# A new schedule for the same 807 operations of a long-convolution block with its feed-forward network

## The chip, the cores and the metric

The kernel runs on one core of a Trainium2 chip. A core has four compute engines with instruction streams of their own, here called PE (TensorE, matmuls out of SBUF into PSUM), ACT (ScalarE), DVE (VectorE) and POOL (GpSimd), and SP (SyncE), which in this kernel only issues DMA transfers. The profile lists PE's weight loads apart, as PEld. The metric is device microseconds of one launch.

## The reference

One sequence of S = 2048 tokens with D = 640 channels, all in bfloat16. Part A is a convolution block in the manner of H3, part B a SwiGLU network of width F = 1728 (`B_x` isn't used).

```python
x   = A_q
lnq = layernorm(x)
k_s = sum over t < 4 of shift(k, 3 - t rows down) * shift_k[:, 3 - t]   # causal, per channel
kv  = k_s * v
y   = irfft(rfft(kv, 4096) * rfft(ssm_k.T, 4096))[:2048] + kv * ssm_D   # per channel
h   = x + lnq * y
n   = layernorm(h)
out = h + (silu(n @ w_gate) * (n @ w_up)) @ w_down
```

## The kernel before

**Tiling.** The sequence is cut into four chunks i = 0 to 3 of 512 tokens, the filter ssm_k into four blocks m likewise. Each is transformed with a DFT matrix (`tab`, 128 rows) by matmuls; the long convolution is the sum of spectral products of chunk and block. `SEQ` names the order in which the tasks are recorded: "P01 K W F0 S1 P11 I1 P02 P12 P03 P13 F1 S2 P22 I2 P23 F2 S3 P33 I3 F3" (P products of chunk and block, I inverse transform, F the feed-forward network (FFN), S the forward side of a chunk, K the fourth filter block, W the FFN's weights).

**Tasks.** The Python code records 807 operations ("tasks") with their reads and writes in a graph `g`; a task's number is the order in which it was recorded. The code gives each a name. Those that matter here:

- k0t / k0e: PE transposes of the first chunk of k and their PSUM evacuations (L528; `evac`, L455 on ACT, L457 or L458 on DVE); tload kT (L450): DMA transposes of the later chunks of k.
- tp, ke, kv: the shift taps as matmuls with diagonals (L732), their evacuation (L455), the product with v (L748, L755). v0 to v3 are the loads of v, x0 to x3 those of q.
- kt / kte, kf / kfe: transposes of the filter to KT and their evacuation; forward transform of the filter (L581) and its evacuation. kb and kc: butterflies and combinations on DVE (L561).
- xf / xfe: forward transform of kv (L581, L619) and its evacuation; p: spectral products (L783); yb: butterflies before the inverse transform (L561, L651).
- iv i.p with a letter: inverse transform of chunk i, position p: the matmuls (L939, L944), e evacuation (L954), g the multiply and add (L961), m and s mean and squares on ACT (L860, L862), v and r the reciprocal deviation (L855 on DVE, L857 on POOL), n the normalised tile (L1001 on DVE).
- ht: the DMA transpose of a normalised tile into hnT, the FFN's input (L450).
- fu and fg i.hg: up and gate matmuls of half h (256 tokens), group g (L1049); sg, su, sv their evacuations (L1057, L1062); mu the product (L1070); dn the down projection (L1135, the last ones split, L1012); gd a copy of its input.
- rs: evacuation of dn (L1151 on ACT, L1152 on DVE), ra: the accumulating DMA that adds it to h, issued by POOL (L568); out: the store, issued by SP (L1164).
- la, lp: small steps of the first layer norm's statistics. UA, GA, UB, GB, PKg, PKu, WdA to WdD: weight loads; itab: the table of the inverse transform.

**Order.** Nothing about order is decided by the graph: `PLAN` holds, for each engine, the list of task numbers that it executes in turn. Each engine runs its list in order, and waits at the head of a task until everything that it depends on is done; whatever stands behind it in the list waits too. SP's list orders the issue of DMAs, so a store whose data isn't ready holds up the transfers behind it.

**PSUM.** There are four PSUM tiles of two banks each. The string `units` in the plan says which of the four each of the successive uses takes. `arrange` then adds, for every use, a wait on the readers of the one that had the tile before:

```python
        for t in self.order["pe"]:
            for pt in t.opens:
                prev = last.get(pt.unit)
                if prev is not None:
                    t.pre |= {x for x in prev.users if x.eng != "pe"}
                last[pt.unit] = pt
```

So a matmul group waits for its data and for the evacuation of the former content of its tile, which ACT or DVE does. `emit` turns dependencies between engines into semaphore waits. A task may run on any engine in its list `engs`; most evacuations may go to ACT or DVE.

Of the kernel before, what the change touches and what calls it, by code (L numbers as in the profile page):

```python
# [50 lines left out]
class _Graph:  # L51
# [131 lines left out]
    def emit(self, block):  # L183
# [74 lines left out]

PLAN = {
# [8 lines left out]
    "act":  # L268
# [9 lines left out]
    "dve":  # L278
# [9 lines left out]
    "pool":  # L288
        "18 16 14 15 128 177 168 161 201 195 186 200 227 229 228 340 285 360 361 398 370 371 289 380 390 293 403 391 381 297 "
        "408 417 419 466 420 525 470 559 474 550 568 478 577 680 584 589 701 706 694 695 635 728 719 639 737 746 643 647 ",  # L290
    "sp":
        "0 2 3 8 4 6 9 7 234 10 12 13 239 300 238 11 230 235 301 233 232 231 299 237 481 179 170 197 188 236 286 482 373 363 "
        "290 294 298 383 650 393 480 467 651 561 552 570 475 471 479 579 649 730 721 640 739 748 644 648 794 800 636 797 803 "
        "806 ",
    "units":
        "0113201022031012033321231021332312133313321010001232312221313201230311022320230103301222001112012120120312322323013103"
        "23101021312302023330210213103130021301200122003201320321302",
    "fills": {
        "wb0": ["zmem", 3],
        "k0t4.0": ["zmem", 1],  # L300
# [945 lines left out]
```

## Time and profile before

| | us |
|---|---|
| three runs | 254.22, 254.73, 254.75 (median 254.73) |
| the profiled execution, whole | 254.13 |
| its span in the profile | 252.2 |

The page of the profile gives the engines' busy time; TensorE's granted clock was full all along. Most of the bytes go out through two kinds of queues: q1, issued by SP, 23.56 MB, and q0, issued by POOL, 13.11 MB. A group in the list of costliest groups has one line of the code, one engine and one operation, with the busy time, the mean of one, and the idle time of the engine just ahead. The largest:

| group | count | busy us | mean ns |
|---|---|---|---|
| L1135 PE matmul (down projection) | 420 | 58.4 | 300 |
| L783 DVE (spectral products) | 29 | 45.1 | 1576 |
| L1049 PE matmul, hnT with GB | 280 | 34.2 | 273 |
| L1057 ACT (activation of the gate) | 32 | 29.0 | 913 |
| L581 PE matmul (forward transforms) | 128 | 19.4 | 300 |

Times of a timeline's row are the start in the span, then the duration; a row with "x4" puts four neighbours of one kind together. A landing time counts from the issue of a DMA to the arrival of its last packet.

### The profile page before, as it was taken

What the parts mean: (1) busy time and instruction counts of PE and PEld (TensorE: products, weight loads), DVE (VectorE), ACT (ScalarE), POOL (GpSimd) and SP (SyncE); (2) the same over time, 40 slices, a digit from 0 to 9 for tenths busy, and PEclk for the clock granted to TensorE, in tenths of its full rate; (3) what the DMA queues carried; (4) which work ended last, traced back from release to release, by engine and by line L of the source; (5) the groups of instructions that cost most, each with busy time, mean ns of one, the idle gap of its engine ahead of it and who ended that gap; (6) DMA issues with size and microseconds to landing.
All of it is one profiled execution on the core that took longest, in us unless ns stands there. A gap on an engine that the chain in (4) does not pass through costs nothing.

```text
span 252.2 us, 5601 instructions
## 1 busy us (share of the span) xinstructions
PE 243.4 (96%) x2405; PEld 190.7 (76%) x2405; DVE 195.5 (78%) x249; ACT 184.7 (73%) x303; POOL 58.7 (23%) x62
## 2 busy tenths in 40 slices
PE   7998997999999999999999999999999999999995
PEld 3776574688887867888888765888886678888763
DVE  2899999999989999999999896989959321312322
ACT  2499999999897994678999699478982856543500
POOL 1000033443113457602103333211141122100000
PEclk9999999999999999999999999999999999999999
DMA  6999999989994465999914718795871144300003
GB/s 212 338 316 222 389 381 292 142 154 169 274 176 78 141 104 109 174 169 216 208 19 76 189 26 82 169 232 99 146 140 26 23 85 79 81 0 3 0 29 104
DMA packets 39063, 37.04 MB, mean 147 GB/s; under 512 B 21235, under 2 KB 34046, under 8 KB 39038
## 3 DMA queue, kind: packets, MB, share of 16 engines
q1 hardware_dynamic: 31648, 23.56, 35.0%
q0 software_dynamic: 7376, 13.11, 30.7%
q8 instruction: 19, 0.31, 0.5%
q14 instruction: 6, 0.05, 0.0%
q10 hardware_dynamic: 14, 0.01, 0.0%
HBM read 16.29 MB, written 2.62 MB: 75 GB/s over the span
## 4 chain that ended last, share of the span: by engine, by line
PE 73%; DVE 11%; DMA 8%; ACT 5%; issue 1%; SPq 0%; DVEq 0%
PE ps L1049 45%; PE ps L1135 18%; PE ps L581 4%; DMA kvo<-in_A_v_dram 3%; DVE C L561 2%; PE ps L944 2%; DVE tt L783 2%; DMA hnT<-qo 2%; PE ps L1012 2%; DMA k0n<-in_A_k_dram 2%; PE ps L732 1%; DVE kvo L755 1%; DVE Y L783 1%; DMA xh<-RB 1%; DVE kvo L748 1%
## 5 line engine op out<-in xcount | busy, mean ns | idle before, releaser
L1135 PE MATMUL ps<-Wd,gu 128*128 128x320 bf16 (+1 forms) x420 | 58.4, 300 | 0.3 <-ACT qo L954 0.3
L1135 PEld LDWEIGHTS ps<-Wd,gu 128*128 128x128 bf16 (+1 forms) x420 | 38.9, 97 | 18.7 <-issue 2.8
L783 DVE TENSOR_TENSOR tt<-XH,C 128x2560 bf16<-128x2560 bf16 (+1 forms) x29 | 45.1, 1576 | 0.2
L1070 DVE TENSOR_TENSOR gu<-gu,ub 128x1024 bf16<-128x1024 bf16 (+1 forms) x32 | 19.9, 621 | 20.9 <-ACT gu L1057 12.9
L1057 ACT ACTIVATE gu<-ps 128x1024 bf16<-128x1024 f32 (+1 forms) x32 | 29.0, 913 | 8.7 <-PE ps L1049 8.5
L1049 PE MATMUL ps<-hnT,GB 128*128 128x256 bf16 x280 | 34.2, 273 | 0.0
L1049 PE MATMUL ps<-hnT,UB 128*128 128x256 bf16 x280 | 33.7, 273 | 0.0
L1062 ACT ACTIVATE ub<-ps 128x1024 bf16<-128x1024 f32 x24 | 24.5, 1020 | 12.4 <-PE ps L1049 9.7
L1049 PEld LDWEIGHTS ps<-hnT,UB 128*128 128x128 bf16 x280 | 27.4, 98 | 3.3
L1049 PEld LDWEIGHTS ps<-hnT,GB 128*128 128x128 bf16 x280 | 27.2, 98 | 3.3
L1049 PE MATMUL ps<-hnT,UA 128*128 128x256 bf16 x240 | 28.8, 273 | 0.0
L1049 PE MATMUL ps<-hnT,GA 128*128 128x256 bf16 x240 | 28.2, 273 | 0.4 <-DMA hnT<-qo 0.4
L1049 PEld LDWEIGHTS ps<-hnT,GA 128*128 128x128 bf16 x240 | 23.4, 98 | 3.5 <-DVE OS L458 0.8
L1049 PEld LDWEIGHTS ps<-hnT,UA 128*128 128x128 bf16 x240 | 23.3, 98 | 3.1 <-ACT XH L455 0.2
L857 POOL TENSOR_TENSOR mv<-mv,half 128x1 f32<-128x1 f32 x16 | 15.7, 982 | 32.9 <-DVE mv L855 28.5
L581 PE MATMUL ps<-KT,tab 128*128 128x320 bf16 x128 | 19.4, 300 | 2.3 <-DVE KT L457 1.1
L860 ACT ACTIVATE qo<-xh 128x640 bf16<-128x640 bf16 x28 | 20.6, 736 | 1.2 <-DMA hnT<-qo 0.5
L954 ACT ACTIVATE qo<-ps,one,st 128x640 bf16<-128x640 f32 x16 | 13.8, 883 | 8.1 <-PE ps L939 7.1
L568 POOL DMA_DIRECT2D xh<-RB x12 | 10.8, 899 | 38.0 <-ACT RB L1151 31.6
L581 PEld LDWEIGHTS ps<-KT,tab 128*128 128x128 bf16 x128 | 11.3, 98 | 8.8 <-DVE KT L457 1.4
L857 POOL TENSOR_TENSOR st<-st,half 128x4 f32<-128x4 f32 x4 | 7.2, 1792 | 38.7 <-DVE st L852 31.4
L862 ACT ACTIVATE qo<-xh,mv 128x640 bf16<-128x640 bf16 x16 | 13.2, 830 | 0.2
(115 smaller groups left out, 377.0 us busy)
## 6 DMA issues: line engine op xcount, KB each, us to landing
C<-US POOLq DMA_DIRECT2D x6, 640.0 KB, 6.6
kc<-in_A_ssm_k_dram SPq DMA_DIRECT2D x4, 640.0 KB, 9.9
xh<-in_A_q_dram SPq DMA_DIRECT2D x4, 640.0 KB, 6.9
out_dram<-xh SPq DMA_DIRECT2D x15, 160.0 KB, 1.9
kvo<-in_A_v_dram SPq DMA_DIRECT2D x3, 640.0 KB, 7.6
xh<-RB POOLq DMA_DIRECT2D x12, 160.0 KB, 2.9
C<-C POOLq DMA_DIRECT2D x2, 640.0 KB, 7.6
Wd<-in_B_w_down_dram SPq DMA_DIRECT2D x1, 1280.0 KB, 11.8
```

What stands on the lines that cost most here:

```text
L568: return g.add(name, "pool", lambda e, n: e.dma_start(dst, src, accum_op=ALU.add, max_dma_last_dim=4096), ("acc", 2 * int(np.prod(dst.shap ...
L581: last = e.matmul(pt.f(c, W), tab[:, f, cs, j], src[:, j, c * W:(c + 1) * W], start=(j == js[0]), stop=(j == js[1]))
L783: g.add(nm, "dve", lambda e, n_: e.tensor_tensor(out=d, in0=a, in1=b, op=op), ("sb", n * D), r=[a, b], w=[d])
L857: g.add(name + "r", "pool", lambda e, n: e.tensor_tensor(out=dst, in0=tmp, in1=hf, op=ALU.pow), ("pp", 4), r=[tmp, half[:]], w=[dst])
L860: g.add(name + "m", "act", lambda e, n: e.activation(out=junk, in_=x, func=ACTF.Identity, scale=-1.0 / D, accum_out=sm), ("aa", D, 0), r=[ ...
L862: g.add(name + "s", "act", lambda e, n: e.activation(out=junk, in_=x, func=ACTF.Square, bias=sm, accum_out=sq), ("aa", D, 1), r=[x, sm], w ...
L954: g.add(nm + "e", "act", lambda e, n, pt=pt, q2=q2, s=s, j=j: e.activation(out=q2, in_=pt.f2(W), func=ACTF.Identity, scale=s[:, 3, j:j + 1 ...
L1049: last = e.matmul(pt.f(q // 2, 256, o=256 * (q % 2)), w[:, c, f0:f0 + P], hnT[:, c, cols], start=(c == 0), stop=(c == NC5 - 1))
L1057: g.add("sg%d.%d%d" % (i, h, gp), "act", lambda e, n, pa=pa, gv=gv, nf=nf: e.activation(out=gv, in_=pa.f(0, 256 * nf).rearrange("p (f x) - ...
L1062: g.add("su%d.%d%d" % (i, h, gp), "act", lambda e, n, pb=pb: e.activation(out=ub[:].rearrange("p b x -> p (b x)"), in_=pb.f(0, 1024), func ...
L1070: g.add("mu%d.%d%d" % (i, h, gp), "dve", lambda e, n, gv=gv, ubv=ubv: e.tensor_tensor(out=gv, in0=gv, in1=ubv, op=ALU.mult), ("sb", 256 * ...
L1135: last = e.matmul(pt.f(c, W), gu[k, fb, col(i, j)], Wd[k, fb, c * W:(c + 1) * W], start=st, stop=sp)
```

## The change

Only `PLAN` is new: the lists of all five engines and `units`. The tasks, their operands, the code that makes them and the fills (PE's filler matmuls) stay. PE's 188 tasks are the same, as are the 64 of SP. Thirteen tasks go to another engine:

| from → to | tasks (number) |
|---|---|
| ACT → DVE | k0e2 (36), k0e4 (37), kf2e.011 (147), gd2.0 (630), xf3e.00 (668) |
| DVE → ACT | k0e0 (35), la2.3x (523), rs2.1 (638), xf3e.20 (672) |
| DVE → POOL | lp0 (129), la2w (526), lp3 (696) |
| POOL → DVE | la3w (695) |

ACT has 247 tasks where it had 248, DVE 248 for 249, POOL 60 for 58.

On SP, UA (231) and v1 (301) stand ahead of itab (11), and GA (230) behind WdB (237). The transpose kT2 (481) moves from ahead of ht0.1 (179) to behind v2 (482). ht0.2 (188) and ht0.3 (197) swap, as do ht1.0 (363) and ht1.1 (373). x2 (480), v3 (651) and kT3 (650) stand behind ht1.3 (393); v3 no longer stands behind the store out1.0 (467), which now goes behind ht2.3 (579). out1.1 (471) stands ahead of ht2.0 (552) and ht2.1 (561), out1.2 (475) ahead of ht2.3, out1.3 (479) ahead of ht2.2 (570), out2.0 (636) ahead of ht3.1 (730). On PE, neighbouring groups are interleaved anew: xf1.110 (317) goes ahead of fu0.00 (241), xf1.101 (323) behind it; iv0.2 (180) goes seven places forward; kf and xf groups swap places. fg2.03 (605), a group of the FFN of chunk 2, goes ahead of xf3.01 and xf3.00 (669, 667). On ACT and DVE the tasks follow: kte3.1 (207), for one, is ahead of kb1.1 (110).

```diff
 PLAN = {
     "pe":
...
-        "93 103 156 99 150 101 107 158 97 105 95 208 302 148 214 171 140 224 162 206 189 144 154 216 146 152 313 311 180 323 "
-        "319 309 315 321 222 212 241 240 245 317 220 210 218 246 251 250 255 265 260 261 275 282 283 354 364 270 266 374 271 "
...
+        "105 150 156 95 158 101 99 93 148 103 107 208 97 302 140 171 214 162 206 189 224 180 154 152 146 144 315 309 313 216 "
+        "311 319 317 222 321 241 323 240 212 245 220 218 210 246 255 251 250 260 265 275 261 282 283 354 364 374 266 270 271 "
...
     "dve":
-        "22 20 35 65 66 68 62 63 39 42 111 119 112 120 113 115 114 116 117 85 118 86 121 46 123 122 59 124 60 87 130 88 125 131 "
-        "132 133 134 135 136 137 127 138 126 308 139 141 173 305 109 164 176 110 207 167 191 178 199 169 160 198 182 203 202 "
-        "194 129 185 204 196 205 187 244 325 226 326 249 342 343 344 345 346 347 348 349 350 254 351 339 259 280 352 397 264 "
...
+        "22 20 36 37 66 65 62 63 68 39 42 111 119 112 113 120 115 114 116 117 85 118 46 121 86 122 123 59 124 60 125 87 127 131 "
+        "130 133 88 132 135 134 137 136 308 138 126 139 141 173 109 305 164 176 207 110 178 167 147 199 191 169 160 198 182 203 "
+        "194 202 185 325 196 204 187 205 226 244 326 249 342 343 344 345 346 348 347 350 349 254 351 339 259 280 352 264 353 "
...
     "sp":
-        "0 2 3 8 4 6 9 7 234 10 12 13 239 300 238 11 230 235 301 233 232 231 299 237 481 179 170 197 188 236 286 482 373 363 "
-        "290 294 298 383 650 393 480 467 651 561 552 570 475 471 479 579 649 730 721 640 739 748 644 648 794 800 636 797 803 "
-        "806 ",
+        "0 2 3 8 4 6 9 7 234 10 12 13 239 300 238 231 301 11 299 233 235 232 237 230 179 170 188 197 236 286 482 481 363 373 "
+        "290 294 383 298 480 393 651 650 471 552 561 475 579 467 479 570 649 636 730 721 739 748 640 648 803 797 794 644 800 "
+        "806 ",
     "units":
-        "0113201022031012033321231021332312133313321010001232312221313201230311022320230103301222001112012120120312322323013103"
-        "23101021312302023330210213103130021301200122003201320321302",
+        "0113201232301103021032120313003212333203120113202300101003313123210311012321201201323122201203123230213210200320321110"
+        "31021232211321020230213310321300132111222323321100132301302",
```

More of the change, by code (lines that the diff above doesn't have):

```diff
@@ L260 @@
     "pe":
[7 rows of a table removed]
-    "act":
[9 rows of a table removed]
-    "dve":
[9 rows of a table removed]
[7 rows of a table added]
+    "act":
[9 rows of a table added]
+    "dve":
[9 rows of a table added]
     "pool":
-        "18 16 14 15 128 177 168 161 201 195 186 200 227 229 228 340 285 360 361 398 370 371 289 380 390 293 403 391 381 297 "
-        "408 417 419 466 420 525 470 559 474 550 568 478 577 680 584 589 701 706 694 695 635 728 719 639 737 746 643 647 ",
+        "18 16 14 15 129 128 177 168 161 201 195 186 200 227 229 228 340 285 360 398 361 370 371 289 380 390 381 293 403 391 "
+        "297 408 417 419 466 420 525 526 470 550 474 559 577 478 568 680 584 589 701 706 694 635 696 728 719 737 639 746 643 "
+        "647 ",
     "sp":
-        "0 2 3 8 4 6 9 7 234 10 12 13 239 300 238 11 230 235 301 233 232 231 299 237 481 179 170 197 188 236 286 482 373 363 "
-        "290 294 298 383 650 393 480 467 651 561 552 570 475 471 479 579 649 730 721 640 739 748 644 648 794 800 636 797 803 "
+        "0 2 3 8 4 6 9 7 234 10 12 13 239 300 238 231 301 11 299 233 235 232 237 230 179 170 188 197 236 286 482 481 363 373 "
+        "290 294 383 298 480 393 651 650 471 552 561 475 579 467 479 570 649 636 730 721 739 748 640 648 803 797 794 644 800 "
         "806 ",
     "units":
-        "0113201022031012033321231021332312133313321010001232312221313201230311022320230103301222001112012120120312322323013103"
-        "23101021312302023330210213103130021301200122003201320321302",
+        "0113201232301103021032120313003212333203120113202300101003313123210311012321201201323122201203123230213210200320321110"
+        "31021232211321020230213310321300132111222323321100132301302",
     "fills": {
```

40 rows, old and new, of the table PLAN are left out of this document.

## The prediction

> **What bounds the kernel now.** I read the page first (span 252.2 us), then the busy time of each engine by stretches.
>
> ```profile
> span 252.2 us, 5601 instructions
> ```
> ```profile
> 0.00:7.38 7.38, 5.57 (x31) 2.86 (x31) 1.57 (x3) 2.57 (x4) 0.90 (x8) 1.00 0.71 225
> 7.38:49.71 42.33, 38.75 (x484) 27.52 (x485) 42.10 (x60) 38.93 (x62) 7.38 (x5) 1.00 1.05 299
> 49.71:150.93 101.22, 101.20 (x1073) 82.12 (x1072) 98.76 (x110) 86.61 (x146) 33.53 (x30) 1.00 0.74 144
> 150.93:157.50 6.57, 5.80 (x41) 3.52 (x41) 4.29 (x8) 6.14 (x14) 2.54 (x4) 1.00 0.82 79
> 157.50:249.54 92.04, 92.03 (x780) 74.72 (x780) 48.18 (x70) 50.46 (x81) 14.33 (x16) 1.00 0.39 82
> ```
>
> In a stretch's row stand its length, the busy time of PE, PEld, DVE, ACT and POOL, the granted clock, the DMA share and the GB/s. PE, the matmul engine, is idle for 8.8 us of the span (252.2 less the five busy times): 1.8 before 7.38, 3.6 up to 49.71, 0.8 between 150.93 and 157.50, and the tail of 252.2 − 249.54 = 2.66. Elsewhere it never stops. Both orders issue the same matmuls and end on the same one, so the change can win at most the 4.4 us of the two holes, and any new wait of PE costs its whole length. In the first hole DVE works 42.1 of 42.3 us and ACT 38.9, so an order that favours one makes another late. Next, the timeline of PE shows what each wait is for.
>
> ```profile
> 34.25 1.25 PE L944 MATMUL ps<-OS,itab 128*128 128x320 bf16 x8 [0.32 <-ACT XT L455]
> ...
> 42.51 1.26 PE L581 MATMUL ps<-KT,tab 128*128 128x320 bf16 x8 [1.05 <-DVE KT L457]
> ...
> 58.44 0.82 PE L1049 MATMUL ps<-hnT,UA 128*128 128x256 bf16 x6
> ...
> 66.63 0.60 PE L1049 MATMUL ps<-hnT,GA 128*128 128x256 bf16 x4
> ...
> 157.50 2.67 PE L1049 MATMUL ps<-hnT,GA 128*128 128x256 bf16 x23 [0.45 <-DMA hnT<-qo]
> ```
>
> PE waits for evacuations of PSUM (L455 on ACT, L457 on DVE), since only four tiles exist, and at 157.50 for the transposed input hnT of chunk 2's FFN.
>
> **The head.** The copy k0e2, which releases the first tap matmuls, goes from ACT to DVE.
>
> ```profile
> 6.30 1.03 ACT kT L455
> ```
> ```profile
> 7.36 1.23 DVE L457 COPY kT<-ps 128x1024 bf16<-128x1024 bf16 x1 [1.78 <-PE ps L528]
> ```
>
> The same shape takes 1.23 on DVE against 1.03, so the taps, which began at 7.38, where the first stretch above ends, begin at 7.58: +0.20. ACT's k0e0 now ends near 8.1, before taps need it at 8.5. The smaller k0e4 runs under the taps. The five products of v behind them on DVE shift alike, and PE's next step with them.
>
> **The first hole.** ACT is the pace from 12 us on.
>
> ```profile
> 24.71 1.40 ACT L455 ACTIVATE KO<-ps 128x640 bf16<-128x640 f32 x2
> ...
> 27.04 0.75 ACT L455 ACTIVATE XT<-ps 128x512 bf16<-128x512 f32 x1
> 27.52 0.87 ACT L455 ACTIVATE C<-ps 128x640 bf16<-128x640 f32 x1
> ...
> 28.69 2.69 ACT L455 ACTIVATE C<-ps 128x640 bf16<-128x640 f32 x4
> 31.02 0.95 ACT L455 ACTIVATE KO<-ps 128x640 bf16<-128x640 f32 x1
> 31.60 1.50 ACT L455 ACTIVATE KT<-ps 128x1280 bf16<-128x1280 bf16 x1
> ...
> 38.21 0.89 ACT L954 ACTIVATE qo<-ps,one,st 128x640 bf16<-128x640 f32 x1
> ```
> ```profile
> 17.62 0.77 DVE L458 TENSOR_SCALAR KO<-ps 128x640 bf16<-128x640 f32 x1
> 18.31 0.48 DVE L847 BATCH_NORM_STATS2 bns<-xh 128x6 f32<-128x320 bf16 x1
> ```
>
> From start to start an evacuation holds ACT (31.02 − 28.69) / 4 = 0.58 us, and DVE 18.31 − 17.62 = 0.69. Between the three KT copies and kte3.0 (31.60) ACT does 11 evacuations and ke1.4 (27.52 − 27.04 = 0.48); the new list has 12, kf2.000's among them, behind KT copies that are 0.23 later: 24.94 + 0.48 + 12 × 0.585 = 32.44 for kte3.0. kf2.000 no longer stands between ke1.0a and ke1.0b, so ke1.0b ends only 0.26 later. On DVE yb0.0 starts with the head's 0.2 and behind kv1.4 (an estimated 0.3); the inverse transform iv0.1, at 34.25 now, follows at 34.8.
>
> The 1.05 us before 42.51 does go: kte3.1, for whose tile PE waited, now stands ahead of kb1.1 on DVE. What is late next is ACT. From iv0.1e (36.1, behind iv0.1) it has 20 tasks up to xf1e.110, whose tile fu0.00 takes: eight of the inverse transforms (four evacuations of the 0.89 above, two means, two squares) at an estimated 0.77 from start to start, eleven evacuations at 0.58, and xf1e.110 at its whole 0.7: 13 us, 49.1. The transpose ht0.0 lands near 49.3 (normalised tile at 46.0 behind kf2e.011 and kc1.s2 on DVE, and the 3.3 us median of the transposes, row below). So fu0.00 starts at 49.3 against 49.71, but five short groups (xf1 and kf3, four matmuls of 0.135 each, 0.54) are left behind it where four are now. To fu0.01, before which both orders have the same work, stand three long groups (2.18 each: 20 matmuls, by the span between 58.44 and 66.63) and these five: 49.3 + 6.5 + 2.7 = 58.6 against 58.44. **+0.15**, the head included. Bounds: −0.4 if hnT and tile are there at once, +0.9 if su0.00 is late, the twelfth ACT task behind xf1e.110 and now the one that frees a tile ahead of fu0.01.
>
> An evacuation that leaves ACT, kf2e.011, costs DVE 0.69 where DVE has no gap; lp0, which leaves DVE, gives back 0.06. So the last two normalised tiles of chunk 0 come later too.
>
> ```profile
> 55.85 3.73 SPq L450 DMA_TRANSPOSE hnT<-qo  x2
> ...
> 57.14 0.44 DVE L1001 TENSOR_SCALAR qo<-xh,mv 128x640 bf16<-128x640 bf16 x1
> ```
> ```profile
> hnT<-qo SPq DMA_TRANSPOSE x1, 3.2
> hnT<-qo SPq DMA_TRANSPOSE x1, 7.5
> hnT<-qo SPq DMA_TRANSPOSE x1, 5.8
> ```
> ```profile
> L450 SPq DMA_TRANSPOSE hnT<-qo x16: 1199/1208/1970, 43.5 to 211.1; - x16
> ...
> DMA to landing us min/median/max: 2.6/3.3/8.2
> ```
>
> The three single issues, ht0.3, ht0.2 and ht2.1, stand with their us to landing; the last fence has the ns that SP's queue is held (minimum, median, maximum) and the landing of all nineteen transposes. Now ht0.3 goes out at 55.85 and lands in 3.2 us, ht0.2 at 57.6 and takes 7.5, beside the accumulating DMAs of POOL. The new SP list has ht0.2 first. iv0.2n starts at 57.14 + 0.63 + 0.3 (kb2.0 behind a later evacuation) = 58.1, so ht0.2 goes at 58.55 and ht0.3, though ready, 1.2 later (the 1208 ns). With 7.5 us each they land at 66.05 and 67.25; the second half of FFN 0 needs both at 66.63 + 0.15 = 66.8. Nothing else is on PE's list there, so the stall is 0 to 1.85 us (the latter if ht0.3 only starts when ht0.2 is done: 66.05 + 2.6). I take **+0.4**, by the 7.5 row. DVE, some 0.5 behind by then, could cost the first FFN's down projection 0.2 of the same 0.4, no more.
>
> The Trainium skill, "DMA: Bandwidth & Descriptors", section "Latency and other measured facts", gives DMA transposes an effective 261 GB/s. A tile of 128x640 bf16 would then pass in an estimated 0.6 us and this term would be 0, the sum 0.4 less; no transpose here lands under 2.6 us.
>
> **The second hole.** It hangs on a chain through SP.
>
> ```profile
> 152.81 4.60 DMA hnT<-qo
> ```
> ```profile
> 149.28 0.88 DVE L1152 TENSOR_SCALAR RB<-ps,st 128x640 bf16<-128x640 f32 x1
> 154.96 2.09 PE L619 MATMUL ps<-kvo,tab 128*128 128x320 bf16 x12
> ```
>
> v3's load stands behind out1.0, which waits for ra1.0; the new list issues it near 120, when xf2 has read the buffer, so kv3.0 waits for it no longer. But iv2.0 hangs on dn1.1 on PE as before. Behind it DVE has yb2.5 and iv2.1g, then rs1.2, which holds DVE until dn1.2 ends (149.28 as now), then xf3e.31 and iv2.0n at 150.8. iv2.1n is queued behind iv2.3g, which waits for ACT's iv2.3e (151.6); it runs at 152.1. So the two transposes go out at 151.3 and 152.6 where they went at 150.9 and 152.81. With the same 4.6 us the last lands at 157.2. PE has then two groups of xf3 left (six took 2.09 less the overlap, 0.27 each): 157.2 + 0.54 = 157.74 against 157.50, **+0.25**. With 2.6 us PE would be the bound at 155.9 and the term −1.05; with the 5.8 that ht2.1 takes now (the third row of issues above), +1.45.
>
> **Costed at nothing.** kT2's transpose moves on SP from before ht0.1 to after v2, where its issue and the longest landing of a transpose, 8.2, end near 92; tp2.4, its reader, comes near 105, and ht1.0, next in the queue, at 95. UA and v1 ahead of itab delay it to an estimated 31 us (1.6 MB in front at the 299 GB/s of the second stretch); iv0.1 needs it at 34.8. out2.0 ahead of ht3.1 waits for ra2.0, five us before ht3.1 is ready. rs2.1, xf3e.20 and xf3e.00 change engine under PE's solid stretch; a mistake there costs PE at most what a tile is late, 0 to 0.4 by my reading of dn2.3 behind gd2.1. The outputs at the end precede the last store, which waits for the last matmul in both.
>
> Sum: 0.15 + 0.4 + 0.25 = +0.8. The profiled execution took 254.13 (1.9 outside its span), so 254.9 by it; the median of the three runs, 254.73, lies 0.6 above that execution and would give 255.5. I predict 255.4, nearer the median.
>
> **Rivals.** *Faster transposes.* At 2.6 to 3.3 us each, as half of them land, the stall at 67 is gone and the second hole gives its 1.05: 0.15 − 1.05 = −0.9, so 0.9 below 254.6 (the forecast less its sum), 253.7. It decides once ht2.1 lands in under 4.4 us, and is whole at 3.3. For it: v3, kT2 and kT3 no longer stand on SP just ahead of these transposes. Against: the slow rows fell beside accumulations of POOL, which stay.
> *Transposes of chunk 0 in series.* The stall of 1.85 with the first hole at +0.9 and the second at +0.25: +3.0, 257.6. For it: the 7.5 row, and the DMA share of 1.05 in the first hole; against: ht0.3's 3.2.
> *The waits only change names.* First hole +0.15, no stall, second hole at 0: 254.6 + 0.15, some 254.8. DVE's 42.1 of 42.3 speaks for it, the added 0.63 on DVE against.
>
> **Chances.** About 0.2%, 0.5 us, is what a measurement of this kernel can tell from no change: 254.2 to 255.2. Forecast 0.42 (its own range 254.9 to 256.2; 0.34 of it beyond the bound), transposes in series 0.24, faster transposes 0.25, names only 0.09. So slower 0.58, the same 0.17, faster 0.25, and a range of 253.4 to 257.4.
>
> **What would show it.** First taps at 7.6; fu0.00 at 49.3 on hnT, and fu0.01 near 58.6; a wait of PE on hnT near 67; no DVE wait on kvo at 144; FFN 2 begun near 157.2 with xf3 left over; no gap of PE elsewhere. fu0.01 before 58, hnT of chunk 2 before 156.5, or a new gap of PE in its two solid stretches would refute a step.

## The result and the profile after

| | before | after |
|---|---|---|
| median, six runs each | 254.47 | 258.53 |
| lowest, highest | 254.09, 255.12 | 257.14, 259.56 |
| the profiled execution, its span | 254.13, 252.2 | 257.14, 255.2 |
| last matmul ends at | 249.53 | 252.50 |

The ratio is 1.015, 95% interval 1.0115 to 1.0185: 1.5% slower, and beyond the range of the prediction. The profiled execution was the fastest of the six; with that of before it makes +3.0 us, while the medians make +4.06. Both differences have to be explained. Here and below, a ratio with its interval leaves out runs more than 1.5% above the fastest of the same kernel, which the medians include.

The page of the changed kernel, then its waits of PE (what it waited for: us in total, times, longest):

```profile
span 255.2 us, 5600 instructions
...
PE 244.1 (96%) x2405; PEld 191.0 (75%) x2405; DVE 195.9 (77%) x248; ACT 184.3 (72%) x302; POOL 64.1 (25%) x64
```
```profile
PE ps L733 <- issue: 1.7, 1, 1.7
...
PE ps L1136 <- DVE gu L1071: 0.9, 1, 0.9
PE ps L1050 <- DMA hnT<-qo: 0.7, 1, 0.7
```

PE is busy as before, so the time went into waits. Line numbers are one higher than before (L733 is the taps, L1050 the up and gate matmuls, L1136 the down projection). The waits stand in PE's timeline:

```profile
48.81 2.36 PE L1050 MATMUL ps<-hnT,UA 128*128 128x256 bf16 x20
...
58.09 1.25 PE L1050 MATMUL ps<-hnT,UA 128*128 128x256 bf16 x10
...
71.04 0.72 PE L1050 MATMUL ps<-hnT,GB 128*128 128x256 bf16 x5 [0.23 <-ACT gu L1058]
...
75.95 3.93 PE L1136 MATMUL ps<-Wd,gu 128*128 128x320 bf16 x28 [0.92 <-DVE gu L1071]
...
106.61 1.88 PE L733 MATMUL ps<-diag,kT 64*128 64x256 bf16 x125
110.16 0.17 PE L733 MATMUL ps<-diag,kT 32*128 32x32 bf16 x1 [1.67 <-issue]
...
135.65 1.88 PE L733 MATMUL ps<-diag,kT 64*128 64x256 bf16 x126 [0.16 <-DMA kT<-in_A_k_dram]
...
159.92 0.27 PE L1050 MATMUL ps<-hnT,GB 128*128 128x256 bf16 x1 [0.74 <-DMA hnT<-qo]
```

In before, the taps of chunk 2 stood in two rows with other work between them (tp2.4, then tp2.0), and PE didn't wait:

```profile
97.25 0.61 PE L732 MATMUL ps<-diag,kT 64*128 64x256 bf16 x14
...
105.94 1.30 PE L732 MATMUL ps<-diag,kT 32*128 32x128 bf16 x112
107.17 2.36 PE L1049 MATMUL ps<-hnT,GB 128*128 128x256 bf16 x20
```

Places with the same work behind them in both kernels give the account, in starts on PE:

| place | before | after | difference | gained or lost since |
|---|---|---|---|---|
| fu0.01 | 58.44 | 58.09 | −0.35 | −0.35 |
| dn0.0 | 74.82 | 75.95 | +1.13 | +1.48 |
| dn1.1 | 140.37 | 143.57 | +3.20 | +2.07 |
| dn2.0 | 186.97 | 189.94 | +2.97 | −0.23 |
| end of the last matmul | 249.53 | 252.50 | +2.97 | 0 |

From start to start a wait costs some 0.16 us more than the idle time in its row, since rows overlap by that much where PE doesn't wait (the row at 58.09 lasts 1.25 us, and the next one starts 1.09 after it): so 0.23 and 0.92 make the 1.48, and 1.67 makes 1.83 of the 2.07. Of the −0.35, 0.19 isn't the order's: the load of k that the first transposes wait for (k0n) landed at 5.41 us in this execution and at 5.60 in that of before.

Both holes, which the prediction looked at most, came out slightly better. The loss sits in the stretch in which PE had never stopped before: at fg0.13 and dn0.0 (0.23 and 0.92 of idle time), and in the middle of the taps of chunk 2, where 125 small matmuls run, PE stands for 1.67 us with "issue" as releaser (nothing that the profile shows), and then does the one that is left.

### The profile page after: what moved, and what is told of

It is laid out like the page before. It is cut to its first block, busy times and chain, and to the rows that moved or that the text cites. A ratio compares the mean times of both kernels' runs of the same rounds, so it can differ in the third digit from the quotient of the medians.

```text
span 255.2 us, 5600 instructions
## 1 busy us (share of the span) xinstructions
PE 244.1 (96%) x2405; PEld 191.0 (75%) x2405; DVE 195.9 (77%) x248; ACT 184.3 (72%) x302; POOL 64.1 (25%) x64
## 4 chain that ended last, share of the span: by engine, by line
PE 61%; DVE 17%; DMA 10%; ACT 7%; issue 3%; SPq 0%; ACTq 0%
PE ps L1050 36%; PE ps L1136 18%; DMA kT<-in_A_k_dram 5%; DMA hnT<-qo 4%; DVE tt L784 3%; DVE C L562 3%; DVE Y L784 3%; PE ps L733 2%; PE ps L945 2%; PE ps L1013 2%; DMA k0n<-in_A_k_dram 1%; ACT qo L863 1%; DVE kvo L756 1%; DVE XH L562 1%; PE ps L620 1%
## 5 line engine op out<-in xcount | busy, mean ns | idle before, releaser
L1136 PE MATMUL ps<-Wd,gu 128*128 128x320 bf16 (+1 forms) x420 | 58.6, 300 | 1.0 <-DVE gu L1071 0.9
L1136 PEld LDWEIGHTS ps<-Wd,gu 128*128 128x128 bf16 (+1 forms) x420 | 38.8, 97 | 20.0 <-issue 3.4
L1058 ACT ACTIVATE gu<-ps 128x1024 bf16<-128x1024 f32 (+1 forms) x32 | 29.0, 916 | 15.6 <-PE ps L1050 15.5
L1050 PE MATMUL ps<-hnT,GB 128*128 128x256 bf16 x280 | 33.7, 273 | 1.0 <-DMA hnT<-qo 0.7
L1050 PE MATMUL ps<-hnT,UB 128*128 128x256 bf16 x280 | 34.2, 273 | 0.0
L1050 PEld LDWEIGHTS ps<-hnT,GB 128*128 128x128 bf16 x280 | 27.2, 98 | 6.6 <-issue 1.9
L1050 PEld LDWEIGHTS ps<-hnT,UB 128*128 128x128 bf16 x280 | 27.3, 98 | 3.2
L1050 PE MATMUL ps<-hnT,UA 128*128 128x256 bf16 x240 | 28.5, 273 | 0.0
L1050 PE MATMUL ps<-hnT,GA 128*128 128x256 bf16 x240 | 28.3, 273 | 0.0
L858 POOL TENSOR_TENSOR mv<-mv,half 128x1 f32<-128x1 f32 x16 | 16.9, 1058 | 41.4 <-DVE mv L856 41.4
L1050 PEld LDWEIGHTS ps<-hnT,GA 128*128 128x128 bf16 x240 | 23.5, 98 | 3.0
L1050 PEld LDWEIGHTS ps<-hnT,UA 128*128 128x128 bf16 x240 | 23.3, 98 | 3.1 <-ACT OS L456 0.2
L582 PE MATMUL ps<-KT,tab 128*128 128x320 bf16 x128 | 20.1, 300 | 1.4 <-ACT KO L456 0.7
L1152 ACT ACTIVATE RB<-ps,st 128x640 bf16<-128x640 f32 x10 | 7.9, 789 | 7.9 <-PE ps L1136 4.8
```

The costliest lines, as they stand in the source:

```text
L582: last = e.matmul(pt.f(c, W), tab[:, f, cs, j], src[:, j, c * W:(c + 1) * W], start=(j == js[0]), stop=(j == js[1]))
L858: g.add(name + "r", "pool", lambda e, n: e.tensor_tensor(out=dst, in0=tmp, in1=hf, op=ALU.pow), ("pp", 4), r=[tmp, half[:]], w=[dst])
L1050: last = e.matmul(pt.f(q // 2, 256, o=256 * (q % 2)), w[:, c, f0:f0 + P], hnT[:, c, cols], start=(c == 0), stop=(c == NC5 - 1))
L1058: g.add("sg%d.%d%d" % (i, h, gp), "act", lambda e, n, pa=pa, gv=gv, nf=nf: e.activation(out=gv, in_=pa.f(0, 256 * nf).rearrange("p (f x) - ...
L1136: last = e.matmul(pt.f(c, W), gu[k, fb, col(i, j)], Wd[k, fb, c * W:(c + 1) * W], start=st, stop=sp)
```

## The experiments

My theory at this point: three places, each with a cause of its own. A task is one block of the graph; where a stall in a task stands behind its first matmul, no semaphore can be the cause, since all waits of a task stand ahead of it. The taps issue 252 instructions (matmuls and weight loads) in 1.9 us, and PE's instructions come by DMA: the page of either kernel has 19 packets, 0.31 MB, on the queue named "instruction" (q8), that is 16 KB for some 253 of PE's 4810 (an estimate, which lays all 19 to PE). So the stall could be a late fetch.

**Is it the place of tp2.4, and is it the fetch?** Before the change tp2.4 ran ahead of dn0.3; now it stands directly ahead of tp2.0 and makes one burst of both.

`tap_early`, from the changed kernel:

```diff
-    pe:  ... 287 291 295 421 422 487 483 431 ...
+    pe:  ... 287 291 487 295 421 422 483 431 ...
-    act: ... 296 423 488 485 ...
+    act: ... 296 488 423 485 ...
```

> The changed kernel with the taps tp2.4 again ahead of dn0.3 on PE, as before the change, instead of directly ahead of tp2.0 (the evacuation ke2.4 ahead of sg1.00, and the PSUM tiles of tp2.4 and fg1.00 swapped). Theory A, in the form that a long run of small matmuls (252 instructions in 1.9 us) outruns the fetch of PE's instructions: the stall of 1.7 us in tp2.0 goes to under 0.4, the time falls by 1.3 to 1.9. Theory B, that the taps wait for data or that the stall is chance: within 0.4 of the changed kernel.

`shift40`, from the changed kernel, no entry of an order moved:

```diff
-    "fills": {"wb0": ["zmem", 3], "k0t4.0": ["zmem", 1]},
+    "fills": {"wb0": ["zmem", 3], "k0t4.0": ["zmem", 1], "dn0.0": ["tab0", 20]},
...
+                    e.matmul(pt.f(0, 64), z[:, 0], z[:, 0, 0:64], start=True, stop=True)
```

> The changed kernel with 20 filler matmuls (64 columns, the table as operand) ahead of dn0.0, in PE's wait there; the order stays. They move every later instruction of PE by 40 places against the 16 KB blocks in which its instructions are fetched. If the fetch is what stalls tp2.0, its block is asked for some 2 us earlier and the stall of 1.7 falls under 0.6: 0.8 to 1.7 us faster, less up to 0.3 that the fillers cost. If tp2.0 waits for data, a tile or a busy DMA ring as such, the stall stays at 1.5 to 1.9 and the time is the same or 0.3 slower.

`tap_late`, from the kernel of before:

```diff
-    pe:  ... 291 487 295 422 421 483 431 ...
+    pe:  ... 291 295 422 421 487 483 431 ...
```

> The kernel of before with one task moved: tp2.4 directly ahead of tp2.0 on PE, as in the changed kernel. Theory A: a stall of 0.8 to 1.9 us inside tp2.0 that no semaphore releases, 255.7 to 256.8; if that stall is also what lets the granted clock fall (0.993 in 6 of 12 runs of the changed kernel, never before), some runs here show it too and lie 1.5 us or more higher. If the stall depends on the DMA traffic of the changed kernel and not on the length of the burst: 254.5 to 255.2.

Medians and ratios to before: tap_early 257.21, 1.0083 (1.0053 to 1.0112); shift40 256.73, 1.0061 (1.0034 to 1.0088), which is 1.8 us under the changed kernel and a little more than I had allowed; tap_late 256.17, 1.0058 (1.0034 to 1.0082) against 254.64, so +1.53 from one moved task. PE's timeline, shift40 first, then tap_late:

```profile
104.83 2.35 PE L1050 MATMUL ps<-hnT,UA 128*128 128x256 bf16 x20
107.11 1.89 PE L733 MATMUL ps<-diag,kT 64*128 64x256 bf16 x126
108.92 2.36 PE L1050 MATMUL ps<-hnT,GB 128*128 128x256 bf16 x20
```
```profile
106.61 1.89 PE L732 MATMUL ps<-diag,kT 64*128 64x256 bf16 x126
109.78 2.36 PE L1049 MATMUL ps<-hnT,GB 128*128 128x256 bf16 x20 [1.28 <-ACT XT L455]
```

In shift40 all 126 matmuls and the FFN behind them run without a stop, though order, data and tiles are those of the changed kernel: what differs is the places of the instructions in their 16 KB blocks, and with them when a block is asked for. In tap_late a stall of 1.28 us appears in the old kernel. Its row names the evacuation ke2.4, but that ended at 107.97, 1.8 us before PE went on, and the stall falls behind PE's 2243rd instruction, in the changed kernel behind its 2241st (those of its sequencer counted), so at the same place but for two. The packets on the instruction queue, from the traces:

| | burst from | packet with the next instructions | PE goes on at | stall |
|---|---|---|---|---|
| before | 105.94 | 104.03 to 105.00 | – | none |
| after | 106.61 | 107.79 to 108.67 | 110.16 | 1.67 |
| shift40 | 107.11 | 102.81 to 104.17 | – | none |
| tap_late | 106.61 | 107.45 to 108.41 | 109.78 | 1.28 |
| ht12_back (below) | 108.14 | 108.90 to 109.78 | 111.21 | 1.20 |

Where the packet lands ahead of the burst there is no stall; where it lands within it, PE goes on 1.4 to 1.5 us behind the packet's end. That settles it for the fetch. How early a block is asked for can be estimated: the last fetches of these traces come some 256 instructions of PE apart, and counted back from them the block is due at about PE's 1953rd instruction, run at 102.2 us before, 104.4 after and 102.8 in shift40. Its packet starts 1.8, 3.4 and 0.1 us later. So shift40 also asked at a moment when the packet came at once; what holds it up in the other two no run takes apart. tap_early brought 0.44 us of another wait at tp2.0, for ke2.4, which my edit had moved on ACT.

**Again, and the waits around dn0.0.** `again` is the changed kernel once more; `ht_swap` puts ht0.3 ahead of ht0.2 as before; `wda_first` puts the load WdA ahead of both.

```diff
-    sp: ... 179 170 188 197 236 286 ...
+    sp: ... 179 170 197 188 236 286 ...      (ht_swap)
+    sp: ... 179 170 236 188 197 286 ...      (wda_first)
```

> The changed kernel once more, for a second trace. Theory A (waits of PE at places that the new order makes: 1.7 us in the middle of the taps of chunk 2, 0.9 at the first down projection, where WdA lands late, 0.7 at the second hole): the same places appear, with lengths that differ by a microsecond or so, and the sum over them follows the time, 257.1 to 259.6. Theory B (no place of its own, transfers that collide here and there): the waits of PE stand at other places in this trace.

> The changed kernel with ht0.3 again ahead of ht0.2 on SP. Theory A: the load WdA, behind both on SP, goes out 2.4 us earlier (60.1 in place of 62.5) and lands before PE needs it at 75.0; the first down projection doesn't wait: 0.8 to 1.2 us faster. Rival: the wait there is for mu0.02 on DVE, which ended at 74.97, and another 0.9 for something else: no change beyond 0.3.

> The changed kernel with the load WdA ahead of ht0.2 and ht0.3 on SP. By theory A, which lays dn0.0's wait of 0.9 us on WdA: it goes out near 58.3, as soon as the last filter transform has read its place, and lands by 73; dn0.0 doesn't wait. ht0.2 and ht0.3 go out 1.5 us later and may land after 66.3, where fg0.10 needs them, or hold ACT's la1.1m: 0.9 faster at best, 0.6 slower at worst. If dn0.0 waited for mu0.02 and not for WdA, its wait stays at 0.9.

again: median 260.54, over the 259.6 that I expected, ratio 1.0139 (1.0094 to 1.0183), with the same places: 1.66 in tp2.0, 0.76 at dn0.0, 0.73 at fg2.03. ht_swap: 258.44, 1.0135 (1.0104 to 1.0165), no gain: the wait at dn0.0 was gone, and fg0.13 ahead of it waited 1.07 in place of 0.23. The chain behind that, in the changed kernel: SP's queue, the landing of WdA, and ACT; then ACT and WdA in ht_swap:

```profile
58.08 4.34 SPq L451 DMA_TRANSPOSE hnT<-qo  x2
62.46 2.04 SPq L448 DMA_DIRECT2D Wd<-in_B_w_down_dram  x1
```
```profile
Wd<-in_B_w_down_dram SPq DMA_DIRECT2D x1, 1280.0 KB, 13.4
```
```profile
64.84 0.74 ACT L861 ACTIVATE qo<-xh 128x640 bf16<-128x640 bf16 x1 [1.62 <-DMA hnT<-qo]
```
```profile
66.58 0.74 ACT L861 ACTIVATE qo<-xh 128x640 bf16<-128x640 bf16 x1 [2.46 <-DMA hnT<-qo]
```
```profile
Wd<-in_B_w_down_dram SPq DMA_DIRECT2D x1, 1280.0 KB, 15.6
```

WdA goes out at 62.46 (59.63 before), lands at 75.86, and dn0.0 starts at 75.95; mu0.02, which the row of PE names, had ended at 74.97. So the wait is WdA's. ht0.2 sets a second one: ACT's la1.1m overwrites the tile that the transpose reads, so ACT stands until it has landed (64.76), and with it the evacuations that free PE's tiles. ht_swap sent WdA out earlier, at 61.01, and it took 15.6 us in place of 13.4; and ht0.2, now second, held ACT 2.46 us. What one gained the other lost. In wda_first dn0.0 doesn't wait, but the transposes behind the load are lost: 275.86 us, ratio 1.0815, since both landed some 21 us after their issue and PE waited 16.4 us for them:

```profile
Wd<-in_B_w_down_dram SPq DMA_DIRECT2D x1, 1280.0 KB, 12.9
...
hnT<-qo SPq DMA_TRANSPOSE x2, 21.4
```

I had allowed 0.6 us for that.

**Which half of the change loses it?** `eng_only` has the new engine orders with the whole SP list of before, `sp_only` the reverse, `eng_tap` is eng_only with the edit of tap_early.

> The changed kernel with the whole SP list of before: new orders on PE, ACT, DVE and POOL, new PSUM tiles, old order of the DMA issues. Theory A puts the 1.7 us in the taps of chunk 2 on PE's order, so it stays; WdA's wait at the first down projection (0.9) and the short wait for kT3 (0.2 to 0.3) come from SP's order and go: 256.0 to 258.0, 1 us faster than the changed kernel. If SP's order makes most of the loss, this comes to 254.5 to 255.5.

> The kernel of before with the new SP list alone. Theory A: 255.5 to 256.5 (WdA late at dn0.0, kT3 late at tp3.4; no stall in tp2.0). If SP's order makes most of the loss: 257 to 259.

> The changed kernel with both undone: tp2.4 ahead of dn0.3 again, and the SP list of before. Theory A: what is left of the change is worth nothing or a few tenths in the first hole, 254.0 to 255.3, and no run shows a mean granted clock under 1.0. If the loss sits elsewhere in the engines' orders: 256 to 257.5.

eng_only: 258.01, ratio 1.012 (1.0082 to 1.0159), with 1.46 of stall in tp2.0 and no wait at dn0.0; its median is just above the range that I expected. eng_tap: 256.31, 1.0056 (1.0035 to 1.0077), over the 255.3 that I gave it: in its trace 0.20 at fg0.13, 0.43 at tp2.0 (for ke2.4 again), 0.17 at dn0.0 and 1.18 at the second hole are left. So the new engine orders are slower than the old ones even without the two losses. From fu0.01 to dn0.0 eng_only's trace loses 0.45 us where the changed kernel's loses 1.48, so SP's order makes 1.0 of that stretch; their medians, 258.01 and 258.53, lie too close to tell the two apart. sp_only missed by far: 269.69, ratio 1.0578. Its PE timeline, then its busy times by stretches (length; PE, PEld, DVE, ACT, POOL; granted clock, DMA share, GB/s):

```profile
131.96 1.04 PE L732 MATMUL ps<-diag,kT 64*128 64x256 bf16 x14 [11.69 <-DMA kT<-in_A_k_dram]
```
```profile
124.60:134.80 10.20, 2.84 (x23) 2.09 (x24) 6.05 (x6) 1.72 (x4) 0.00 (x0) 0.50 0.81 130
```

In the new SP list kT3 stands behind v3, which waits until 123 us for the last reader of its buffer. The old PE order wants kT3 at 120.3 and PE stands 11.7 us; the new one does tp3.4 at 135.5, where kT3 has just landed (135.51, 12.1 us after its issue at 123.39). So the new SP list doesn't fit the old PE order, and fits the new one with nothing to spare; the new orders run with the old list too (eng_only).

**Why do half of the runs lie higher?** Six of the twelve runs of the changed kernel (two of the first six, four in again) have a mean granted clock of 0.993 or 0.987 over the span; ht_swap has three in six. Before has none, nor eng_only (6 runs), eng_tap or tap_late (12 each). One candidate was kT3's narrow landing, another the length of the stall in tp2.0, to which ht1.2 may contribute: it moved ahead of out0.3 and runs from 103.56 to 113.01, beside the fetch.

```diff
-    sp: ... 480 393 651 650 471 ...
+    sp: ... 480 393 650 651 471 ...          (kt3_first; kt3_tap too)
-    pe: ... 291 295 421 422 487 483 431 ...
+    pe: ... 291 295 487 421 422 483 431 ...  (kt3_tap, with 488 ahead of 423 on act)
-    sp: ... 290 294 383 298 480 ...
+    sp: ... 290 294 298 383 480 ...          (ht12_back)
```

`tap_ht12` is tap_late with ht1.2 (383) ahead of out0.3 (298).

> The changed kernel with the transpose kT3 ahead of the load v3 on SP, which waits until 123 us for the last reader of its buffer. Theory A: kT3 lands near 123 in place of 135.5, so that tp3.4 never waits; no run has a mean granted clock of 0.993 (6 of 12 had it in the changed kernel), the spread of the runs shrinks to some 2 us, and the median falls to 257.0 to 257.9, the stall of 1.7 us in tp2.0 staying. Rival: the low clock comes from that stall in tp2.0 and stays in about half of the runs, median 258 to 260.

> The same, and tp2.4 on PE behind dn0.3 and ahead of fg1.00 and fu1.00, so that 40 matmuls of the FFN stand between it and tp2.0 (ke2.4 ahead of sg1.00 on ACT). Theory A: no stall over 0.4 us in tp2.0, 255.3 to 256.3; what is left against before is WdA's wait (0.8 to 1.1 us at dn0.0) and the second hole. If more than these places carries the loss: over 256.5.

> The changed kernel with the transpose ht1.2 again behind the store out0.3 on SP, so that it starts near 111 us and not at 103.6, beside the fetch of PE's instructions at 107.8. Theory C: the fetch waits behind ht1.2's packets (9.5 us to landing there), and where it waits long enough PE's idle time makes the granted clock fall. Then no run shows 0.993, the stall in tp2.0 is 1.2 to 1.6 as in eng_only and tap_late, and the median is 256.8 to 257.8. If ht1.2 has no part in it: 0.993 in two or more of the runs, median 258 to 260.

> The kernel of before with the two entries that theory C names and nothing else: tp2.4 directly ahead of tp2.0 on PE (tap_late), and ht1.2 ahead of out0.3 on SP. Theory C: a stall of 1.5 us or more in tp2.0, a mean clock of 0.993 in a quarter or more of the runs (tap_late had none in 12), median 256.5 to 258.5. If ht1.2 has no part: as tap_late, 256.2, all runs at 0.999 or more.

kt3_first: 258.06, ratio 1.013 (1.0085 to 1.0175); the trace has kT3 at 126.46, and two of six runs still show 0.993: kT3 is not the cause. kt3_tap: 256.63, 1.0095 (1.0064 to 1.0126), over the 256.3 that I expected, no run under 1.0; of the 1.11 us that its tp2.0 waits, up to 107.88, none is the fetch (packet landed at 107.51, and PE is still some 220 instructions ahead of the place of the stall): ACT held ke2.4, which my edit put ahead of sg1.00, until DVE had read its target, and sg1.00, which PE's row names, ended only at 107.83.

```profile
ACT XT L456 <- DVE C L784: 2.9, 1, 2.9
```

ht12_back: the stall is 1.20 in place of 1.67 and all six runs have 0.999 or more, as expected; but its median, 258.15 (ratio 1.0122, 1.0083 to 1.0161), is over the 257.8 I gave it. From fu0.01 to the last matmul its trace takes 193.94 us, that of the changed kernel 194.41, which is the shorter stall; the rest of its excess lies ahead of fu0.01 (59.73 against 58.09; see the last section). All four traces with a stall of 1.66 or more have ht1.2 early and all four of 1.20 to 1.46 have it late, which agrees with a share of ht1.2 and doesn't prove it. tap_ht12: 256.11, 1.0067 (1.004 to 1.0093), no 0.993. It tested nothing: in the old ACT order the tile for ht1.2 is ready only at 110.3, so the transpose went out at 110.35 in either place.

What the clock does stands in the trace of wda_first, which has the taps of the changed kernel. PE's timeline and the stretches behind the stall:

```profile
127.86 0.17 PE L733 MATMUL ps<-diag,kT 32*128 32x32 bf16 x1 [1.66 <-issue]
127.97 4.03 PE L1050 MATMUL ps<-hnT,GB 128*128 128x256 bf16 x20
```
```profile
126.20:127.80 1.60, 0.01 (x1) 0.00 (x0) 1.60 (x2) 0.00 (x0) 0.00 (x0) 1.00 0.49 76
...
128.40:131.80 3.40, 3.40 (x18) 2.41 (x17) 1.76 (x2) 2.53 (x3) 0.00 (x0) 0.50 1.11 230
131.80:135.20 3.40, 3.40 (x31) 2.96 (x30) 3.37 (x4) 2.27 (x3) 0.00 (x0) 0.99 0.22 26
```

Half a microsecond after the stall the granted clock falls to 0.50 for 3.4 us, and 20 matmuls that take 2.36 us elsewhere take 4.03. That is 1.7 us a time, and 3.4 × 0.5 of a span of 256 is the 0.7% by which 0.993 lies under 1. The Trainium skill, "TensorE: Matmul & The Clock Gate", section "Part 1: The HAM clock gate (the "warmup" mystery)", has the gate judge PE's activity over free-running windows of 3413 ns; the stretch of 3.4 us agrees, and so do the moments at which the clock changes in this trace, 70.41, 87.47, 128.43 and 131.84 us: they lie 5, 12 and 1 times 3.413 apart. A window that lies at chance would explain why the same stall costs this in one execution and not in the next. That is argued and not shown: the other four traces with a stall of 1.66 to 1.74 us (the changed kernel, again, ht_swap, kt3_first) have the full clock throughout. Over all executions of these four kernels the low clock came in 11 of 24, over those of the four whose trace has a stall of 1.20 to 1.46 (eng_only, tap_late, ht12_back, tap_ht12) in none of 32; how long the stall was in the runs without a trace isn't known. Two runs of shift40 and one of tap_early had a low clock without that stall in their trace; what set it there is open.

Nor is the low clock the whole difference. In again its three runs at 0.993 took 259.84, 261.24 and 262.25, those at full clock 257.28 and 258.59: two of the three lie further above these than 1.7 us. Of the changed kernel's first six, the four at full clock have a median of 257.95, 3.5 over before: so the low clock makes 0.6 of the +4.06, the waits in the trace make 3.0, and the 0.5 between is of the size by which executions scatter (last section), but isn't taken apart.

**Is there a version that beats both?** From the kernel of before: `v3_early` issues v3 ahead of out1.0, `mix` adds kte3.1 ahead of kb1.1 on DVE.

```diff
-    sp:  ... 393 480 467 651 561 ...
+    sp:  ... 393 480 651 467 561 ...
-    dve: ... 164 176 110 207 167 ...
+    dve: ... 164 176 207 110 167 ...         (mix alone)
```

> The kernel of before with one entry of SP's list moved: v3 ahead of the store out1.0. By the chain of waits kv3.0 waited 0.69 us for v3 at 145 and PE 0.45 for hnT at 157: the second hole shrinks by 0.3 to 0.7, 254.0 to 254.5. If the hole hangs on dn1.1 and rs1.2 as I argued in the prediction, there is no change: 254.5 to 254.9.

> v3_early, and on DVE the evacuation kte3.1 ahead of kb1.1, as in the changed kernel (the PSUM tile that PE waits 1.05 us for at 42.5). Theory: 0.4 to 1.0 us of the first hole go, 253.2 to 254.2. If ACT or the transposes of chunk 0 are late next, the hole comes back behind it: as v3_early.

v3_early 254.12, ratio 0.9997 (0.9974 to 1.0019); mix 254.42, 0.9987 (0.9969 to 1.0005): neither can be told from before by its runs. In v3_early's trace the stretch from dn1.1 to dn2.0 is 0.35 us shorter than before, in mix's 0.34: v3 had a share in the second hole, too small for the runs to show. In mix PE's wait of 1.05 us moved from kf2.011 to 1.25 at kf2.110, the next group: the first hole goes from name to name.

## Why the prediction was wrong

Two steps failed: the place at 67 us, priced at +0.4, lost 1.48, and what was costed at nothing lost 2.07. "Elsewhere it never stops" held for the old order, and the new one stops at 71, 76, 110 and 135.6 us. The other terms came within 0.5.

**The head (+0.20): right.** The taps began at 7.39, where 7.58 was forecast, but only because k0n landed 0.19 us earlier in that execution. DVE's copy starts 0.69 behind this landing, as ACT's did 0.70 behind it (6.30 and 5.60):

```profile
6.10 1.82 DVE L458 COPY kT<-ps 128x1024 bf16<-128x1024 bf16 x2 [0.45 <-PE ps L529]
...
7.39 0.84 PE L733 MATMUL ps<-diag,kT 64*128 64x256 bf16 x18 [0.36 <-DVE kT L458]
```

From the landing to the first tap are 1.98 us against 1.78. The other traces say the same: 1.77 to 1.81 in the six with the old head, 1.97 or 1.98 in the eleven with the new.

**The first hole (+0.15): 0.3 too high, inside its bounds.** fu0.00 began at 48.81 and fu0.01 at 58.09, −0.35; counted from the landing of k0n, fu0.01 comes at 52.68 against 52.84, so −0.16. The step's own terms also add up a little lower than it has them (49.3 + 6.5 + 2.7 is 58.5), which is 0.1 of this; which of the others was too high stays open.

**The place at 67 us (+0.4): right place, wrong victim.** The step said that the second half of FFN 0 waits for ht0.2 and ht0.3 and that "nothing else is on PE's list there". They landed at 64.76 and 65.65, in time for fg0.10 at 66.28. What I didn't price is what else hangs on them: WdA behind them on SP (0.92 at dn0.0) and ACT's la1.1m (0.23 at fg0.13). From fu0.01 to dn0.0 the loss is 1.48. SP's list showed WdA (236) directly behind the two transposes: it goes out at 62.46 in place of 59.63, and DVE's delay, for which the step allowed 0.2, isn't what PE waits for.

**The second hole (+0.25): right chain, 0.5 too high.** −0.23 from dn1.1 to dn2.0. The transposes left as the step has them, behind dn1.1 and rs1.2: at 154.42 and 155.71, which is 151.2 and 152.5 less the 3.20 by which dn1.1 was late, where the step has 151.3 and 152.6. The term that was off is the landing: 4.13 us for the last in place of 4.6. PE's 0.74 of wait replaces 0.45 + 0.26. The step gave v3 no share; v3_early's trace gives it 0.35.

**"Costed at nothing": the step that failed most.** Two entries. tp2.4 was looked at only for its data (kT2, "near 92", read "near 105"), which held; its new neighbour was not looked at, and the burst of 252 instructions cost 1.83 us from start to start in tp2.0, and, if the counts above mean what they suggest, the drop of the clock in half of the runs. The row of tp2.0 in before, 112 matmuls in 1.30 us, showed that taps issue at a rate like no other task, and the page showed instructions on a DMA queue; nothing in the trace of before shows a stall by it. And kT3 behind v3 was not mentioned, though the step follows v3 to "near 120, when xf2 has read the buffer": whatever is queued behind a waiting DMA waits too. It cost 0.16 here, and 11.7 where PE's order didn't allow for it.

The rival of the transposes in series gave 257.6, close to the profiled 257.14, but for a wait that didn't occur. The range ended at 257.4, below even that rival, to which the prediction gave 0.24; and no wait in it was of a kind of which the trace of before had no example, as the stall in the taps is.

## What to carry to other kernels

When an order is changed, look at each engine's neighbours as well as at its dependencies: many tiny instructions in a row (here 252 in 1.9 us) use up the instructions that have been fetched, and the next block comes by a DMA, by the estimate above 0.1 to 6.0 us after it is due. Spread such tasks among long ones, and check the fetch against the burst in the trace. On a DMA queue, price the entry behind the moved one: a load that lands with 0.1 us to spare, or a transpose behind a big load, is where a microsecond or twenty appear. And a schedule is one object: the same SP list costs 11.7 us of wait beside one PE order and 0.16 beside another.

## What was not expected of the hardware

- An instruction block for PE (16 KB) is asked for and served like any transfer. By the estimate above, counted back in steps of 256 instructions, one due at 71.7 us in the changed kernel came at 77.70, 6.0 us later.
- In wda_first a stall of 1.66 us, with 1.2 us of small taps ahead of it, was enough for 3.4 us at half the clock, where I would have looked for a longer pause. It doesn't always do it: in ht_swap's trace 1.74 us left the clock full.
- Two DMA transposes issued behind a 1.3 MB load, beside three accumulating transfers, took some 21 us to land; ahead of it the same two took 5.6 and 6.7.
- The first taps take 2.47 us in some executions and up to 4.43 in others, with either order at the head; v3_early and before:

```profile
7.58 4.43 PE L732 MATMUL ps<-diag,kT 64*128 64x256 bf16 x70
```
```profile
7.38 2.47 PE L732 MATMUL ps<-diag,kT 64*128 64x256 bf16 x70
```

This is some 2 us of scatter that no order made, and it goes with the clock. The record of the granted clock starts, at full, at 7.31 us in the trace of before, at 10.22 in tap_late's and at 11.85 in v3_early's (ahead of its start the views print 1.00 with nothing recorded); the first taps take 2.47, 3.81 and 4.43 us, and fu0.01, up to which these three kernels are the same, starts at 58.44, 59.30 and 60.18. In the changed kernel's trace the record starts at 7.18, so the +3.0 is free of it; in ht12_back's at 11.26 and in eng_only's at 11.19. It may be most of the 2.5 us over which 23 runs of before spread (253.56 to 256.03), which their times alone can't show. A profiled execution has to be read with it.
